# Linear attention and feed-forward layers on one core: another order for every engine's queue

## Chip, core and metric

The kernel runs on one NeuronCore of a Trainium2 chip. The time is what the device takes for one execution, in microseconds (us); several executions are timed and the median is given. Lower is better. The core's engines work side by side, each through a queue of its own in program order: TensorE (PE, with its weight loads as PEld), VectorE (DVE), ScalarE (ACT), GpSimd (POOL), and SyncE (SP), which here issues nearly all transfers.

## The reference

Two kinds of layer alternate, A, B, A, B, on 2048 tokens of width 512 in bf16; both A layers share weights, both B layers too.

```python
def _A_ref(x, wqkv, wo):          # 32 heads of 16
    q, k, v = ...                 # x @ wqkv
    phi = lambda t: jnp.where(t > 0, t + 1, jnp.exp(t)) + 1e-6
    pq, pk = phi(q), phi(k)
    kv = jnp.einsum("bhsd,bhse->bhde", pk, v)
    z = jnp.einsum("bhsd->bhd", pk)
    num = jnp.einsum("bhqd,bhde->bhqe", pq, kv)
    den = jnp.einsum("bhqd,bhd->bhq", pq, z)[..., None] + 1e-6
    ...                           # (num / den) @ wo

def _B_ref(x, w1, w2):            # 512 -> 1376 -> 512
    ...                           # relu(x @ w1) @ w2

x = x + _A_ref(_layernorm(x, axis=-1), A_wqkv, A_wo)
x = x + _B_ref(_layernorm(x, axis=-1), B_w1, B_w2)
x = x + _A_ref(_layernorm(x, axis=-1), A_wqkv, A_wo)
x = x + _B_ref(_layernorm(x, axis=-1), B_w1, B_w2)
```

## The kernel before

The 2048 tokens are 16 tiles of 128, in four chunks of four tiles. Layers are numbered 0 (A), 1 (B), 2 (A), 3 (B), and the steps of a layer are interleaved with those of the next, so that a later layer starts on chunk 0 while the earlier one still works on chunk 3.

A step has a name with the numbers of layer, chunk or tile, and part. In the first A layer a tile goes through `bnst`, `bnag` (statistics, VectorE, lines 846 and 847), `rstd`, `fnorm` (normalization, VectorE, line 884), `trp` (transposition on TensorE, line 913) or `tr` (transposition by DMA, line 899), and `trev` (its copy to SBUF). `kproj`, `qh` and `qproj` are the projections, all issued as matmuls at line 952. `lin` and `exp` (lines 932 and 934, ScalarE) and `em` and `phi` (VectorE) make the feature map. `den`, `lnd`, `rdc`, `spread` (DMA, line 1226) and `pqs` make the division; `g`, `kv`, `kvmask`, `m` and `fin` contract keys with values and apply the output weights; `resid`, `sq`, `nmean` to `nbias` and `norm` are the residual and the next normalization. Many products are computed with seven block products instead of eight: `aqsum` and `aksum` (VectorE, line 1005) subtract blocks of the weights; `q7` and `k7` are the seven products of the projections, `h1` to `h7` and `p1` to `p7` those of the two feed-forward matrices, with the sums of the other operand in `as`, `hs` and `ssum`. In a feed-forward layer `hv` are ScalarE's copies of half-made sums out of PSUM (line 699 seeds a second PSUM bank with such a copy), `hc` the additions and relus, `hr` the last 96 hidden units, `trh` their transposition.

The order of work is not the order of the code. All steps are first collected in a graph, and a planner then makes one queue for each engine. In the graph a step gets a number as it is created, and its place in the queue is that number plus a hint from a table, line 421:

```python
op.prio = op.idx + HINTS.get(op.key, 0)
```

`HINTS` (line 63) has 1,638 such numbers. It has another 264 entries that end in "!": these choose, for a step that two engines could do, one of them. The planner's window is 1 on every engine (line 60), so a queue is simply sorted by place, and a step that waits holds up all that stand behind it. The planner then runs its queues against its own table of durations to find when each of the eight PSUM banks comes free, gives the banks out, and derives the waits from that. `LOAD_LATE` (line 53) is what it adds to the landing times of the early loads in that calculation.

The places that the prediction uses are sums of this kind. On VectorE `bnst4` was created as number 52 and has the hint 17, place 69; `aqsum3` was created as 200 and has -44, place 156. The TensorE steps of the first microseconds stand in this order before: `kproj1_1`, `qh0_0_1_0`, `trp2`, `qh0_0_2_0`, `trp3`, `qh0_0_3_0`, `qh0_0_0_0`, `kproj2`, four `qh` steps, `qh0_0_2_1`, `kproj3`, two `qh` steps, `trp4`.

Of the kernel before, what the change touches and what calls it, by code (L numbers as in the profile page):

```python
# [52 lines left out]
LOAD_LATE = {"x1": 270.0, "x2": 440.0, "wka": 580.0, "wkb": 440.0, "wqa": 600.0, "x4": 1200.0, "wqb": 1160.0, "x12": 960.0, "x8": 760.0, "wv0": 350.0}  # L53
# [9 lines left out]
HINTS = {"0.aqsum1": -69, "0.aqsum1!": 0, "0.aqsum2": -40, "0.aqsum2!": 0, "0.aqsum3": -44, "0.aqsum3!": 0, "0.aqsum4": -12,  # L63
# [327 lines left out]
class _Graph:  # L391
# [19 lines left out]
    def add(self, eng, emit, reads=(), writes=(), dur=100.0, lat=0.0, dma=False, name=""):  # L411
        if eng == ACT and name != "table" and not dma:
# [7 lines left out]
                   POOL: 0 if name.startswith(("ms_", "as", "onec")) else 2 if "norm" in name else 1}  # L420
        op.prio = op.idx + HINTS.get(op.key, 0)
        deps = {}
# [29 lines left out]
    def add_flex(self, alts, reads=(), writes=(), name=""):  # L452
        e0, em0, d0 = alts[0]
        op = self.add(e0, em0, reads, writes, d0, name=name)
        op.alts = list(alts)
        c = HINTS.get(op.key + "!")
        if c is not None and c < len(alts):
# [1516 lines left out]
```

## Time and profile before

| | us |
|---|---|
| median of 3 runs | 263.93 |
| lowest and highest | 262.88, 264.66 |
| the profiled execution | 262.89 |
| its span, first to last instruction | 260.9 |

The profile is of one execution. It lists for each engine when each instruction ran. A line of the timeline gives the start, the time until the last record of the group ends, engine, source line, operation, what is written and read, sizes and count; in brackets stands the idle time before it and what ended it. Matmul records overlap, since the next matmul starts before the last one has drained, so the distance between two starts tells more than the length of a record. The chain is followed back from the last instruction: at each step to what released it.

### The profile page before, as it was taken

How to read it: one execution, taken by the hardware profiler on the slowest of the kernel's cores; microseconds unless marked ns; L12 is line 12 of the kernel's file. 1: busy time of each engine (PE TensorE's matmuls, PEld its weight loads, DVE VectorE, ACT ScalarE, POOL GpSimd, SP SyncE). 2: the span in 40 equal slices, each digit the busy share in tenths (PEclk: the TensorE clock that was granted, in tenths of full speed). 3: DMA queues.
4: the chain of work that ended last, by engine and by line, in shares of the span. 5: the costliest groups of instructions: out<-in, count | busy, mean ns of one | idle time of the engine just before them, and what ended most of it. 6: DMA issues, size and time to landing. Idle time of an engine off the chain costs nothing.

```text
span 260.9 us, 5905 instructions
## 1 busy us (share of the span) xinstructions
PE 255.5 (98%) x2176; PEld 198.3 (76%) x2176; DVE 231.1 (89%) x574; ACT 204.1 (78%) x442; POOL 60.4 (23%) x164
## 2 busy tenths in 40 slices
PE   7999999999999999999999999999999999999995
PEld 2555668734778888898888878774488988988884
DVE  4899999799989999999899999759999999977674
ACT  4899998769989978899998799686999945970200
POOL 4110000018843016340330340002986000000000
PEclk9999999999999999999999999999999999999999
DMA  6757970743432440323021030047442504300104
GB/s 198 285 143 126 322 230 0 186 111 67 85 68 57 60 83 8 75 41 63 0 58 26 0 75 9 3 107 174 92 80 57 102 3 123 60 20 3 80 3 161
DMA packets 45980, 22.46 MB, mean 86 GB/s; under 512 B 35872, under 2 KB 44416, under 8 KB 45952
## 3 DMA queue, kind: packets, MB, share of 16 engines
q1 hardware_dynamic: 45680, 21.83, 34.7%
q8 instruction: 17, 0.28, 0.5%
q10 hardware_dynamic: 272, 0.26, 0.4%
q14 instruction: 11, 0.09, 0.1%
HBM read 7.14 MB, written 2.10 MB: 35 GB/s over the span
## 4 chain that ended last, share of the span: by engine, by line
PE 82%; ACT 6%; DMA 5%; DVE 2%; SPq 2%; issue 2%
PE ps L952 81%; DMA Tb<-xn 3%; ACT sqscr L967 2%; SPq L1226 2%; ACT xn L894 1%; DMA xin<-in_A_x_dram 1%; DMA big<-rdc 1%; PE ps L913 1%; ACT ps L699 1%; ACT rdc L1216 0%; ACT lnd L1214 0%; DVE xn L889 0%; DVE xn L884 0%; DVE bst L846 0%; DVE big L1234 0%
## 5 line engine op out<-in xcount | busy, mean ns | idle before, releaser
L699 ACT ACTIVATE ps<-ps 128x512 f32<-128x512 f32 (+1 forms) x41 | 23.1, 573 | 19.4 <-PE ps L952 17.8
L952 PE MATMUL ps<-big,xn 128*128 128x256 bf16 (+1 forms) x224 | 32.7, 288 | 0.0
L952 PE MATMUL ps<-w,big 128*128 128x256 bf16 (+1 forms) x256 | 32.5, 272 | 0.0
L967 ACT ACTIVATE sqscr<-xres 128x512 bf16<-128x512 f32 x48 | 29.8, 622 | 2.9 <-DVE xres L959 2.2
L952 PE MATMUL ps<-Mf,big 128*128 128x512 bf16 x128 | 28.5, 379 | 0.0
L952 PEld LDWEIGHTS ps<-w,big 128*128 128x128 bf16 (+1 forms) x256 | 25.0, 98 | 3.0
L952 PEld LDWEIGHTS ps<-big,xn 128*128 128x128 f16 x224 | 21.3, 98 | 6.6 <-issue 1.1
L952 PE MATMUL ps<-Tb,w 128*128 128x256 f16 x160 | 24.2, 273 | 0.0
L952 PEld LDWEIGHTS ps<-Mf,big 128*128 128x128 bf16 x128 | 12.2, 98 | 14.6 <-ACT Mf L1165 0.5
L1435 DVE TENSOR_TENSOR big<-ps,escr 128x512 bf16<-128x512 f32 (+1 forms) x38 | 22.5, 600 | 0.9 <-PE ps L952 0.5
L952 PE MATMUL ps<-xn,xin 128*128 128x256 f16 x160 | 23.0, 273 | 0.1
L952 PE MATMUL ps<-xn,w 128*128 128x256 f16 x160 | 22.9, 273 | 0.0
L868 POOL TENSOR_SCALAR mean<-s 128x2 f32<-128x2 f32 x24 | 8.9, 377 | 54.9 <-DVE xres L959 53.7
L952 PE MATMUL ps<-wqkv,Tb 128*128 128x512 bf16 (+1 forms) x96 | 20.6, 344 | 0.0
L1423 ACT ACTIVATE big<-ps 128x512 bf16<-128x512 f32 (+1 forms) x37 | 20.2, 563 | 0.3 <-DVE xn L1401 0.2
L894 ACT ACTIVATE xn<-xres,nbias,rstd 128x512 f16<-128x512 f32 x24 | 19.5, 830 | 0.5 <-DVE nbias L878 0.5
L1454 ACT ACTIVATE escr<-ps 128x512 f32<-128x512 f32 (+1 forms) x38 | 19.2, 541 | 0.4 <-PE ps L952 0.2
L876 POOL TENSOR_TENSOR rstd<-veps,nhalf 128x2 f32<-128x2 f32 x24 | 18.0, 750 | 4.5 <-DVE veps L874 4.0
L952 PE MATMUL ps<-w,Tb 128*128 128x96 bf16 (+2 forms) x176 | 17.3, 224 | 0.2 <-DMA Tb<-xn 0.2
L952 PEld LDWEIGHTS ps<-Tb,w 128*128 128x128 bf16 x160 | 15.5, 98 | 2.2 <-DVE w L1383 0.3
L952 PEld LDWEIGHTS ps<-xn,w 128*128 128x128 bf16 x160 | 15.5, 98 | 2.0
L952 PEld LDWEIGHTS ps<-xn,xin 128*128 128x128 bf16 x160 | 15.2, 98 | 2.2 <-ACT ps L699 0.4
(146 smaller groups left out, 627.8 us busy)
## 6 DMA issues: line engine op xcount, KB each, us to landing
big<-rdc SPq DMA_DIRECT2D x32, 128.0 KB, 2.7
xin<-in_A_x_dram SPq DMA_DIRECT2D x3, 512.0 KB, 7.5
w<-in_B_w_dram SPq DMA_DIRECT2D x1, 1376.0 KB, 7.1
w<-in_B_w_dram SPq DMA_DIRECT2D x1, 1280.0 KB, 10.5
wqkv<-in_A_wqkv_dram SPq DMA_DIRECT2D x3, 256.0 KB, 5.0
wqkv<-in_A_wqkv_dram SPq DMA_DIRECT2D x1, 512.0 KB, 4.3
wo<-in_A_wo_dram SPq DMA_DIRECT2D x1, 512.0 KB, 4.3
out_dram<-GT SPq DMA_DIRECT2D x1, 512.0 KB, 2.6
```

Of the source, the lines that this page charges most:

```text
L699: g.add(ACT, lambda e: e.activation(psv[:, b, 0:w], psv[:, src, 0:w], ACTF.Identity), [("ps", src)], [("ps", b)], C_ACT_PSUM if w == 512 e ...
L868: g.add(POOL, lambda e: e.tensor_scalar(mean[:, sl], s1[:, sl], -INV_D, None, ALU.mult), [("s1", i) for i in tl], [("mean", i) for i in tl ...
L876: g.add(POOL, lambda e: e.tensor_tensor(rstd[:, sl], veps[:, sl], nhalf[:, 0:n], ALU.pow), [("veps", lo), ("nhalf",)], [("rstd", i) for i ...
L894: (ACT, lambda e: e.activation(xn[:, i, :], src, ACTF.Identity, scale=rstd[:, i:i + 1], bias=nbias[:, i:i + 1]), C_ACT_SB_AP)],
L913: last = e.transpose(psb()[:, 128 * c:128 * c + 128], xn[:, i, 128 * c:128 * c + 128], ident[:])
L952: last = e.matmul(o, l, r, start=st, stop=sp, skip_group_check=skip)
L967: g.add(ACT, lambda e: e.activation(sqscr[:, q, :], xres[:, i, :], ACTF.Square, scale=math.sqrt(INV_D), accum_out=s2[:, i:i + 1]), xr(i), ...
L1226: dma(lambda e, j=j, u=u: e.dma_start(unit_ap(u), rdc[32 * j:32 * j + 32, t, :].unsqueeze(1).broadcast_to([32, 4, 512])), [("rdc", t)], [( ...
L1423: g.add_flex([(ACT, lambda e: e.activation(ap, src(), ACTF.Relu), C_ACT_PSUM if w == 512 else 270.0), (DVE, lambda e: e.tensor_scalar(ap, ...
L1435: g.add(DVE, lambda e: e.tensor_tensor(ap, sh(psv[:, bank, 0:w]), sh(other()), ALU.add), [("ps", bank)] + okeys + ([] if first else bk), q ...
L1454: g.add(ACT, lambda e, w=w: e.activation(q[:, 0:w], psv[:, bank, 0:w], ACTF.Identity), [("ps", bank)], key, C_ACT_PSUM if len(cs) == 2 els ...
```

## The change

Only two tables are changed: `LOAD_LATE`, and the numbers in `HINTS`. The keys of the tables are the same; 1,418 of the 1,638 place numbers and 50 of the 264 choices of engine differ. No instruction is added or removed; 50 small steps (evacuations, relus, additions, parts of the normalization) go to the other engine that can do them. Cut to what the prediction speaks of:

```diff
-LOAD_LATE = {"x1": 270.0, "x2": 440.0, "wka": 580.0, "wkb": 440.0, "wqa": 600.0, "x4": 1200.0, "wqb": 1160.0, "x12": 960.0, "x8": 760.0, "wv0": 350.0}
+LOAD_LATE = {"x1": 320.0, "x2": 490.0, "wka": 780.0, "wkb": 540.0, "wqa": 1000.0, "x4": 1300.0, "wqb": 1260.0, "x12": 1060.0, "x8": 960.0, "wv0": 350.0}
...
-HINTS = {"0.aqsum1": -69, "0.aqsum1!": 0, "0.aqsum2": -40, "0.aqsum2!": 0, "0.aqsum3": -44, "0.aqsum3!": 0, "0.aqsum4": -12,
+HINTS = {"0.aqsum1": -43, "0.aqsum1!": 0, "0.aqsum2": -24, "0.aqsum2!": 0, "0.aqsum3": -126, "0.aqsum3!": 0, "0.aqsum4": 36,
...
-         "0.qc7_3_22_exp": -14, "0.qh0_0_0_0": -43, "0.qh0_0_0_1": -10, "0.qh0_0_1_0": -59, "0.qh0_0_1_1": -36,
+         "0.qc7_3_22_add": -21, "0.qc7_3_22_exp": -14, "0.qh0_0_0_0": -54, "0.qh0_0_0_1": -6, "0.qh0_0_1_0": -63,
...
-         "1.h5_0_0": 18, "1.h5_0_2": 12, "1.h5_0_4": 19, "1.h5_1_0": 7, "1.h5_1_2": -5, "1.h5_1_4": -10, "1.h5_2_0":
+         50, "1.h4_3_2": 60, "1.h4_3_4": 60, "1.h5_0_0": 18, "1.h5_0_2": 11, "1.h5_0_4": 18, "1.h5_1_0": -8,
...
-         "1.hc11_3_2!": 0, "1.hc11_3_4": 61, "1.hc11_3_4!": 0, "1.hc12_0_0": 37, "1.hc12_0_2": 45, "1.hc12_0_4": 52,
+         "1.hc12_0_0": 34, "1.hc12_0_2": 38, "1.hc12_0_4": 52, "1.hc12_1_0": 26, "1.hc12_1_2": 28, "1.hc12_1_4": 37,
...
-         "1.hs1_1": -18, "1.hs1_2": -52, "1.hs1_3": -120, "1.hs2_0": 26, "1.hs2_1": -9, "1.hs2_2": -25, "1.hs2_3":
+         "1.hrrelu2!": 0, "1.hrrelu3": 4, "1.hrrelu3!": 0, "1.hs1_0": 18, "1.hs1_1": -13, "1.hs1_2": -47, "1.hs1_3":
...
-         -96, "2.q7_2_2": -60, "2.q7_2_3": -33, "2.q7_2_4": 1, "2.q7_2_5": -46, "2.q7_2_6": -42, "2.q7_2_7": -11,
+         "2.q7_2_3": -38, "2.q7_2_4": 0, "2.q7_2_5": -45, "2.q7_2_6": -42, "2.q7_2_7": -22, "2.q7_3_1": -75,
```

Sorted by the new places, the first TensorE steps read `qh0_0_1_0`, `kproj1_1`, `qh0_0_0_0`, `trp2`, `trp3`, `qh0_0_3_0`, `kproj2`, seven `qh` steps, `kproj3`, `qh0_0_2_1`, `trp4`: the same number of matmuls ahead of `trp4`. VectorE reads `bnst4`, `aqsum3`, `bnag4`, `fnorm6`, `veps4`, `fnorm7`, `bnst5`, `fnorm4`. On SP the four spreads of chunk 0 stand ahead of the load `w2b` and the transposition of chunk 2's first half ahead of `trh0`; the loads up to x8 keep their order. The first steps of TensorE up to `kproj1_0`, and of VectorE up to `bnst4`, are unchanged.

593 rows, old and new, of the table HINTS are left out of this document.

## The prediction

> **What bounds the kernel now.** I read the page's busy shares first, then the chain that ended last, then the windows by stage, and then the timeline of TensorE alone at each place where the chain leaves it.
>
> ```profile
> span 260.9 us, 5905 instructions
> PE 255.5 (98%) x2176; PEld 198.3 (76%) x2176; DVE 231.1 (89%) x574; ACT 204.1 (78%) x442; POOL 60.4 (23%) x164
> L952 PE MATMUL ps<-Mf,big 128*128 128x512 bf16 x128 | 28.5, 379 | 0.0
> ```
> ```profile
> 76.00 73.59 PE ps L952 x690
> ...
> 151.34 3.48 DMA Tb<-xn
> 154.81 0.05 issue
> 154.86 103.43 PE ps L952 x924
> 258.29 0.02 issue
> 258.32 0.42 DVE rdc L1609
> ```
> ```profile
> 16.00:42.00 26.00, 26.00 (x170) 15.97 (x170) 25.92 (x71) 26.00 (x57) 0.56 (x3) 1.00 0.68 193
> 217.00:258.00 41.00, 41.00 (x396) 36.58 (x395) 32.42 (x64) 15.44 (x33) 0.00 (x0) 1.00 0.22 59
> ```
>
> A busy share of 98% proves little, since matmuls overlap in the records: the mean record of the 512-column form is 379 ns, while 128 of them fill only 28.5 us, 223 ns each. So I go by the distance from one start to the next. The last leg of the chain is 924 matmuls in 103.43 us, 112 ns each, without one step off the engine. The windows (PE, PEld, DVE, ACT and POOL busy, then granted clock, DMA) say the same at a clock of 1.00. They also show that from 16 to 42 us VectorE (25.92 of 26.00) and ScalarE (26.00) have nothing left either, while from 217 to 258 us both have room. TensorE is the bound; an order of queues can only win where TensorE waits.
>
> **How much waiting there is.** The spacings first, then the waits. TensorE from 8 to 14 us:
>
> ```profile
> 8.32 0.38 PE L952 MATMUL ps<-Tb,wqkv 128*128 128x256 f16 x2
> 9.09 0.40 PE L913 MATMUL ps<-ident,xn 128*128 128x128 f16 x4 [0.38 <-DVE xn L884]
> 9.32 0.38 PE L952 MATMUL ps<-Tb,wqkv 128*128 128x256 f16 x2
> 9.54 0.39 PE L913 MATMUL ps<-ident,xn 128*128 128x128 f16 x4
> 9.76 0.60 PE L952 MATMUL ps<-Tb,wqkv 128*128 128x256 f16 x4
> 10.20 1.03 PE L952 MATMUL ps<-wqkv,Tb 128*128 128x512 bf16 x4
> 11.06 1.25 PE L952 MATMUL ps<-Tb,wqkv 128*128 128x256 f16 x10
> 12.15 1.03 PE L952 MATMUL ps<-wqkv,Tb 128*128 128x512 bf16 x4
> 13.02 0.60 PE L952 MATMUL ps<-Tb,wqkv 128*128 128x256 f16 x4
> 13.65 0.40 PE L913 MATMUL ps<-ident,xn 128*128 128x128 f16 x4
> ```
>
> Ten matmuls of 256 columns lie between 11.06 and 12.15: 0.109 us each. Four of 512 lie between 12.15 and 13.02: 0.217 each. By these the pair at 8.32 is issued by 8.54 and the next step, `trp2`, starts at 9.09: a wait of 0.55. The four at 13.02 are out by 13.46 and `trp4` starts at 13.65: 0.19. The later waits, first the two around 75 us (TensorE, then VectorE, then ScalarE), then those near 154 and near 52 us (TensorE, and VectorE's step between):
>
> ```profile
> 74.04 0.38 PE L952 MATMUL ps<-Tb,w 128*128 128x256 f16 x2
> 74.63 0.84 PE L952 MATMUL ps<-w,Tb 128*128 128x96 bf16 x16 [0.21 <-DMA Tb<-xn]
> 75.30 0.60 PE L952 MATMUL ps<-Tb,w 128*128 128x256 f16 x4
> 76.00 0.83 PE L952 MATMUL ps<-xn,xin 128*128 128x256 f16 x6
> ```
> ```profile
> 74.51 0.42 DVE L1401 TENSOR_TENSOR xn<-Tb 128x512 f16<-128x512 f16 x1 [0.87 <-DMA Tb<-xn]
> 74.86 0.68 DVE L1435 TENSOR_TENSOR big<-ps,escr 128x512 bf16<-128x512 f32 x1
> ```
> ```profile
> 75.58 0.37 ACT L699 ACTIVATE ps<-ps 128x256 f32<-128x256 f32 x1 [0.73 <-DVE big L1435]
> ```
> ```profile
> 153.77 1.03 PE L952 MATMUL ps<-big,xn 128*128 128x512 bf16 x4
> 154.86 0.61 PE L952 MATMUL ps<-Tb,wqkv 128*128 128x256 f16 x4
> ```
> ```profile
> 52.18 0.59 PE L952 MATMUL ps<-Mf,big 128*128 128x512 bf16 x2
> 52.86 0.60 PE L952 MATMUL ps<-wo,KVT 128*128 128x512 bf16 x2
> ```
> ```profile
> 52.38 0.42 DVE L1158 TENSOR_TENSOR KVT<-ps,bmask 128x256 bf16<-128x256 f32 x1 [0.34 <-PE ps L952]
> ```
>
> In the same way: `hr1_0` waits 74.63 - 74.26 = 0.37 for the transposed chunk; `h6_0_4` waits 76.00 - 75.74 = 0.26 for ScalarE's copy at 75.58, which waited for VectorE's addition at 74.86, which stood behind `hs1_1`, which waited 0.87 for the same transposition; `q7_3_1` waits 154.86 - 154.64 = 0.22 for the transposition issued at 151.34; `m2` waits 52.86 - 52.61 = 0.25 for `kvmask1`. Together 0.55 + 0.19 + 0.37 + 0.26 + 0.22 + 0.25 = 1.84 us. That is all that I find worth the name, and it is 0.7% of 262.89: a new order that removed every one of them would not be faster by 1%.
>
> **The change part by part.** Nothing is added or removed; every price is a wait that goes, moves or appears. `LOAD_LATE` emits nothing: it only feeds the planner's clock, and reaches the program through the banks and the waits it chooses.
>
> *The start, SP and loads.* The order of the ten loads is the same, so x and the weights should land as before. On TensorE `qh0_0_0_0` moves from behind `trp3` to ahead of `trp2` (its place number falls from 62 to 51): two matmuls, 0.22 us, go into the wait of 0.55. That saves nothing by itself, because the next wait down the queue, `trp4` at 13.65, is set by VectorE:
>
> ```profile
> 9.70 1.29 DVE L846 BATCH_NORM_STATS2 bst<-xin 128x6 f32<-128x512 bf16 x2 [0.35 <-DMA xin<-in_A_x_dram]
> 11.12 0.66 DVE L846 BATCH_NORM_STATS2 bst<-xin 128x6 f32<-128x512 bf16 x1
> 11.82 0.18 DVE L847 BATCH_NORM_AGGREGATE mv<-bst 128x2 f32<-128x6 f32 x1
> 12.60 0.68 DVE L846 BATCH_NORM_STATS2 bst<-xin 128x6 f32<-128x512 bf16 x1
> 13.20 0.40 DVE L884 TENSOR_SCALAR xn<-xin,mv,rstd 128x512 f16<-128x512 bf16 x1
> ...
> 17.62 0.41 DVE L1005 TENSOR_TENSOR Mf<-wqkv 128x512 bf16<-128x512 bf16 x1
> 17.96 1.05 DVE L884 TENSOR_SCALAR xn<-xin,mv,rstd 128x512 f16<-128x512 bf16 x3
> ```
>
> From the landing of x4 (9.70) to `fnorm4` (13.20 to 13.60) VectorE has no gap, and `trp4` follows 0.05 behind. Into this run the change puts `aqsum3` (place 156 before, 74 after; `bnst4` 68, `bnag4` 77). The trace has its twin at 17.62, whose successor starts 0.34 later. So `fnorm4` ends at 13.94 and `trp4` starts at 13.99: +0.34. Queued behind `aqsum3` are `bnag4`, `fnorm6`, `fnorm7` and the transposition of their tiles, all later by the same 0.34, so nothing there is lost twice. TensorE has as much work ahead of `trp4` as before, so it cannot pay this back; it only waits longer (0.19 + 0.22 + 0.34 = 0.75). Bounds: nothing, if in a usual run x4 lands so that a hole is there for `aqsum3`; 0.41, its whole record. I take +0.34.
>
> *16 to 42 us.* VectorE is rid of that 0.34, TensorE had no wait to lose, no engine choice flips here. I take 0. The cover is the two full engines beside it; the price if it tears is the second rival.
>
> *42 to 60 us.* The one `fin` step between `kv1_3` and `m2` is exchanged for another (`fin2_0` for `fin0_0`), both two matmuls, and `kvmask1` keeps its place: the 0.25 stays. The spreads of the first chunk now pass `ld_w2b` on SP, whose data are first read far later: 0. `m0` comes closer to `kvmask0`, two steps of four 256-column matmuls (0.87) behind `kv0_3`, where the `m2` row shows that 0.43 + 0.25 = 0.68 are needed: 0.
>
> *74 to 76 us.* Ahead of `hr1_0` stand the same steps as before and `norm6` keeps its neighbours: 0.37 stays. But `hc12_0_2` now stands ahead of `hs1_1` on VectorE (517 against 525; before 524 against 520), so its 0.87 holds up nobody, and on TensorE `h5_1_0` (536) passes `h6_0_4` (539): four matmuls, 0.44, more than the wait. -0.26. SP puts `trh0` behind a transposition of chunk 2; its reader `p1_0_0` comes some fifteen TensorE steps later, and I take 0.
>
> *149 to 155 us.* `q7_2_7` (place 62 before, 51 after) goes ahead of `q7_3_1`: 0.44 of work in front of a wait of 0.22; the queue that makes the transposition is in the same order. -0.22. *The last layer* is shuffled as much as the rest, but its final VectorE steps and stores are the same in kind, and the 0.42 at 258.32 stays the end.
>
> Named terms: +0.34 - 0.26 - 0.22 = -0.14. Beside them, some hundreds of steps trade places and 50 small steps change engine. That exposes waits which no row shows, since each depends on banks and evacuations. From below: none (it cannot gain where TensorE has no gap). From above: as many as the old order has after 16 us (four: 0.25, 0.37, 0.26, 0.22, together 1.10). Two of those four are dissolved here; I take it that two others replace them, at their mean of 0.28, and halve the 0.55 since the last stage has room on both other engines: +0.3. Sum: +0.16, call it +0.2.
>
> Against the profiled run: 262.89, of which 260.9 is the span and 2.0 lies around it, gives 263.1. The median of the runs, 263.93, stands 1.04 above the profiled run; the trace does not say where, so I leave that distance as it is: **264.1**.
>
> **The rivals.**
> *Almost all waits go:* the named gains count, the start costs nothing because x4 lands in another rhythm, and 74.63 shrinks too: -0.26 - 0.22 - 0.37 = -0.85, 263.1; at the very best -1.84, 262.1. For it: the waits are few and small. Against: the gapless VectorE run from 9.70. Chance 0.16.
> *VectorE or ScalarE loses time between 16 and 42 us:* one queue's head waits for a product or a transposition that now comes later, and with 25.92 and 26.00 of 26.00 busy nothing regains it. The price of one such wait is the 0.87 of `hs1_1`; three chunks are evacuated in this stage, 3 x 0.87 = 2.6, so 266.7. It decides from the point where the idle time exceeds the 0.34 that `aqsum3` leaves free. Against: TensorE has no gap at all there now. Chance 0.12.
> *TensorE's spacing itself gives way* beside other neighbours. If the 128 matmuls at 223 ns went at the 109 ns of half their width, 128 x 0.114 = 14.6 us would go: 249.5. Against: both spacings hold wherever no wait is shown. Chance 0.02. The Trainium skill, "TensorE: Matmul & The Clock Gate", section "Back-to-back issue gap", gives about 131 ns a matmul for a sustained stream of 512 columns; the 217 ns between 12.15 and 13.02 disagree, and the trace decides.
> *The change does nothing:* the moved steps lie under cover everywhere, 263.9. Chance 0.08. The forecast has the remaining 0.62.
>
> **How the numbers follow.** 1% is 2.6 us, about what a measurement of this kernel can tell from no change. Faster by that needs the spacing rival: 0.02, and 0.01 for what no case covers. Slower: the second rival, 0.12. Within: 0.85. The forecast's own range is 263.4 (no new wait, start +0: -0.48) to 265.0 (start +0.41, all 1.10 of new waits: +1.03). To hold 8 in 10 it takes in the first rival, down to 262.7, and the smaller half of the second, up to 265.8.
>
> **What would show it.** Right: `trp4` at about 14.0 behind a longer wait, no TensorE gap before the step that was `h6_0_4` and before `q7_3_1`, one of about 0.37 still before `hr1_0`, 0.25 before `m2`. Wrong: `trp4` still at 13.65; a gap in TensorE between 16 and 42 us; several new gaps of over 0.3 after 80 us; or a chain whose last leg is no longer TensorE alone.

## The result, and the profile after

| us | before | after |
|---|---|---|
| median of 9 runs each | 263.61 (262.67 to 264.95) | 262.21 (261.68 to 262.97) |
| ratio of the runs, 95% interval | | 0.9945 (0.9919 to 0.997) |
| again, 29 and 12 runs on another occasion | 263.09 (262.32 to 264.76) | 262.42 (261.60 to 263.28) |
| ratio, 95% interval | | 0.9959 (0.9935 to 0.9983) |
| the profiled execution, its span | 262.89, 260.9 | 262.21, 260.5 |

The change is faster by 0.4 to 0.55% (the ratios take all runs; the medians are 1.40 and 0.67 us apart), and its executions lie closer together. The forecast, 264.1 with 262.7 as its lower end, missed it; that the difference would stay under 1% held. The two profiled executions differ by only 0.68 us, of which 0.4 lie in the span. So part of the gain may lie in executions of the kernel before that its first profile does not show.

The page of the changed kernel, its chain of waits around 70 us and its windows (PE, PEld, DVE, ACT and POOL busy, granted clock, DMA):

```profile
span 260.5 us, 5888 instructions
PE 255.3 (98%) x2176; PEld 198.9 (76%) x2176; DVE 230.7 (89%) x574; ACT 207.5 (80%) x446; POOL 60.0 (23%) x160
```
```profile
70.18 4.40 DMA Tb<-xn
74.58 0.14 issue
74.71 183.07 PE ps L953 x1674
257.79 0.02 issue
257.81 0.43 DVE rdc L1610
```
```profile
16.00:42.00 26.00, 26.00 (x172) 15.79 (x170) 25.70 (x69) 25.90 (x56) 0.67 (x3) 1.00 0.65 190
```

TensorE is the bound as before. Its last unbroken leg is now 183 us long and starts at `hr1_0`, behind a DMA transposition of 4.40 us; before, the leg began at 154.86. Between 16 and 42 us the two full engines stayed full and TensorE kept its pace. TensorE at the four places of the prediction (the start, near 52, near 74 and near 154 us), then VectorE's run from the landing of x4:

```profile
8.23 0.38 PE L953 MATMUL ps<-Tb,wqkv 128*128 128x256 f16 x2
8.78 0.72 PE L914 MATMUL ps<-ident,xn 128*128 128x128 f16 x8 [0.16 <-DVE xn L885]
...
13.17 0.38 PE L953 MATMUL ps<-Tb,wqkv 128*128 128x256 f16 x2
13.39 0.39 PE L914 MATMUL ps<-ident,xn 128*128 128x128 f16 x4
...
51.87 0.59 PE L953 MATMUL ps<-Mf,big 128*128 128x512 bf16 x2
52.55 0.61 PE L953 MATMUL ps<-wo,KVT 128*128 128x512 bf16 x2
...
73.70 0.38 PE L953 MATMUL ps<-xn,w 128*128 128x256 f16 x2
74.71 0.84 PE L953 MATMUL ps<-w,Tb 128*128 128x96 bf16 x16 [0.64 <-DMA Tb<-xn]
75.39 0.60 PE L953 MATMUL ps<-Tb,w 128*128 128x256 f16 x4
75.83 0.82 PE L953 MATMUL ps<-xn,xin 128*128 128x256 f16 x6
...
153.96 1.03 PE L953 MATMUL ps<-big,xn 128*128 128x512 bf16 x4
154.82 0.60 PE L953 MATMUL ps<-Tb,wqkv 128*128 128x256 f16 x4
```
```profile
9.18 1.29 DVE L847 BATCH_NORM_STATS2 bst<-xin 128x6 f32<-128x512 bf16 x2
...
10.61 0.66 DVE L847 BATCH_NORM_STATS2 bst<-xin 128x6 f32<-128x512 bf16 x1
11.18 0.41 DVE L1006 TENSOR_TENSOR Mf<-wqkv 128x512 bf16<-128x512 bf16 x1
11.51 0.17 DVE L848 BATCH_NORM_AGGREGATE mv<-bst 128x2 f32<-128x6 f32 x1
...
12.88 0.40 DVE L885 TENSOR_SCALAR xn<-xin,mv,rstd 128x512 f16<-128x512 bf16 x1
```

By the distances from start to start: the wait before `h6_0_4` is gone (75.83 follows 75.39 by 0.44, the time of four matmuls), so is the one before `q7_3_1` (0.86 for four of 512 columns), and 0.25 before `m2` stays. But `hr1_0` now waits 74.71 - 73.92 = 0.79, where 0.37 was to stay. And `aqsum3` stands where the prediction put it, at 11.18, yet `trp4` starts at 13.39, not at 14.0 (x4 also landed earlier here, at 9.16 in place of 9.68).

### The profile page after: what moved, and what is told of

Same layout as the page of the kernel before. It is cut to its first block, busy times and chain, and to the rows that moved or that the text cites. A ratio compares the mean times of both kernels' runs of the same rounds, so it can differ in the third digit from the quotient of the medians.

```text
span 260.5 us, 5888 instructions
## 1 busy us (share of the span) xinstructions
PE 255.3 (98%) x2176; PEld 198.9 (76%) x2176; DVE 230.7 (89%) x574; ACT 207.5 (80%) x446; POOL 60.0 (23%) x160
## 4 chain that ended last, share of the span: by engine, by line
PE 85%; ACT 5%; DVE 4%; DMA 4%; SPq 1%; issue 1%
PE ps L953 84%; DVE xres L960 2%; DMA Tb<-xn 2%; SPq L1227 1%; ACT sqscr L968 1%; DMA big<-rdc 1%; DMA xin<-in_A_x_dram 1%; ACT xn L895 1%; DVE bst L847 1%; PE ps L914 0%; ACT rdc L1217 0%; DVE big L1235 0%; ACT escr L935 0%; ACT ps L700 0%; ACT lnd L1215 0%
## 5 line engine op out<-in xcount | busy, mean ns | idle before, releaser
L953 PE MATMUL ps<-big,xn 128*128 128x256 bf16 (+1 forms) x224 | 32.1, 288 | 0.0
L869 POOL TENSOR_SCALAR mean<-s 128x2 f32<-128x2 f32 x24 | 7.2, 301 | 54.4 <-DVE xres L960 52.8
L1424 ACT ACTIVATE big<-ps 128x512 bf16<-128x512 f32 (+1 forms) x38 | 18.9, 527 | 0.4 <-PE ps L953 0.3
L1445 ACT ACTIVATE big<-big 128x1024 bf16<-128x1024 bf16 (+1 forms) x16 | 14.3, 904 | 3.5 <-DVE big L1436 3.3
```

Of the source, the lines that this page charges most:

```text
L869: g.add(POOL, lambda e: e.tensor_scalar(mean[:, sl], s1[:, sl], -INV_D, None, ALU.mult), [("s1", i) for i in tl], [("mean", i) for i in tl ...
L953: last = e.matmul(o, l, r, start=st, stop=sp, skip_group_check=skip)
L1424: g.add_flex([(ACT, lambda e: e.activation(ap, src(), ACTF.Relu), C_ACT_PSUM if w == 512 else 270.0), (DVE, lambda e: e.tensor_scalar(ap, ...
L1445: g.add_flex([(ACT, lambda e: e.activation(row, row, ACTF.Relu), 945.0 if len(cs) == 2 else C_ACT_SB), (DVE, lambda e: e.tensor_scalar(row ...
```

## The experiments

Waits of TensorE below are distances from start to start, less the usual one for the width (217 ns for 512 columns, 109 for 256, 42 for 96). Each kernel was also timed beside the kernel before, if not called a profiled run alone.

**Where does the gain sit, and was the first profile of before a typical one?** Two kernels with half of the new numbers each, and a second profiled run of each of the pair, without an edit.

```diff
-"0.aqsum1": -69
+"0.aqsum1": -43
...
-"1.h5_1_0": 7
+"1.h5_1_0": -8
...
 "2.q7_2_7": -11
 "2.q7_3_1": -78
```

That is the first, with the new numbers for layers 0 and 1 and the old ones for 2 and 3; the second is the reverse.

> The first two layers take the new order, the last two keep the old one; nothing is computed otherwise. Theory A (the gain is a wait here and there, spread over the kernel): about half of the gain, 0.5 to 0.8 us faster than before, and the wait near 154 us before q7_3_1 is still there with 0.2 us. Theory B (the old order loses time in a usual execution near the start, where transfers land at changing times, and the profiled execution of before was a lucky one): nearly the whole gain, 1.0 to 1.4 us faster. Theory C (the gain lies in the last two layers, whose order changed as much): within 0.3 us of before.

> The last two layers take the new order, the first two keep the old one; nothing is computed otherwise. Theory A: 0.4 to 0.8 us faster than before. Theory B: only the wait of 0.22 us before q7_3_1 goes, 0.1 to 0.3 us faster. Theory C: 1.0 to 1.4 us faster.

> The kernel before, unchanged, for a second profiled execution. Theory B: the loads land at other times than in the first profile by some tenths of a us, and the waits of TensorE come out larger than the 1.84 us found there, by up to 0.8 us. Theories A and C: the same waits within 0.2 us.

> The changed kernel, unchanged, for a second profiled execution. Theory B: its waits vary less from profile to profile than those of the kernel before, within 0.4 us in sum. Theories A and C: as little as those of the kernel before.

New orders in layers 0 and 1 alone: 263.72 us, ratio to the kernel before 1.0026 (1.0002 to 1.005). In layers 2 and 3 alone: 267.23 us, 1.0159 (1.0123 to 1.0195). Neither half carries the gain, and both are slower than either whole. TensorE in the second, where the steps of layer 1 in their old order meet layer 2 in its new one:

```profile
120.48 1.27 PE L952 MATMUL ps<-w,big 128*128 128x256 bf16 x10 [0.80 <-ACT ps L699]
...
127.33 0.39 PE L952 MATMUL ps<-w,big 128*128 128x256 bf16 x2 [0.94 <-DVE xres L1601]
```

Neither wait is in the kernel before or after. The first half, too, has a wait that neither whole has, 0.78 us near 145.6. So these two runs suggest that the order of one layer is made for that of the next, and say nothing about where the gain lies.

The second profiles said more. The kernel before took 264.35 us, 1.46 more than in its first profile, the changed one 263.17. The start, where theory B looked for the loss, is not the place: `trp4` started at 13.67 in this profile of the kernel before, at 13.65 in the first. The chain of waits of this second profile of the kernel before, and TensorE there:

```profile
70.72 5.36 DMA Tb<-xn
```
```profile
74.30 0.38 PE L952 MATMUL ps<-Tb,w 128*128 128x256 f16 x2
76.21 0.84 PE L952 MATMUL ps<-w,Tb 128*128 128x96 bf16 x16 [1.53 <-DMA Tb<-xn]
```

The transposition that `hr1_0` waits for landed 5.36 us after its issue, 4.05 in the first profile, and the wait was 1.69 us, not 0.37. That is nearly the whole difference between the two executions. What delays it shows in the DMA queues. From 70 to 75 us, first the first profile of before, then this one (queue, kind: packets, MB, share of the time of 16 DMA engines):

```profile
q8 instruction: 1, 0.02, 1.7%
q14 instruction: 1, 0.01, 0.4%
```
```profile
q14 instruction: 1, 0.01, 2.1%
q8 instruction: 1, 0.02, 1.1%
```

These are blocks of the program itself, fetched while it runs: 16 KB on one queue, 8 KB on the other. The 8 KB block took 0.3 us in the first profile (0.4% of 80 us) and 1.65 us in the second, where its packet starts 0.26 us after that of the 16 KB block, which took 0.89. In the first profile it came first. Both fall on the packets of the transposition, which run from 1.2 us after its issue. This became theory F: TensorE's wait depends on when two instruction fetches come.

**Moving TensorE's fetches.** The warm-up matmuls at the start were cut into more, narrower ones of the same total width, so that TensorE's instructions are counted on but no queue changes its order. The changed kernel was timed again beside them.

```diff
-                for k in range(WARM):
-                    last = e.matmul(psv[:, wt, :], wrm[:, 0:128], wrm[:, :], start=True, stop=True)
+                for w in [112] * 32 + [128] * 4:
+                    last = e.matmul(psv[0:64, wt, 0:w], wrm[:, 0:64], wrm[:, 0:w], start=True, stop=True)
```

With 16 more matmuls the list is `[168] * 16 + [176] * 8`.

> The changed kernel once more, timed beside the kernel before on one chip. Theory F (instruction fetches): around 72 us TensorE's 16 KB instruction fetch and an 8 KB fetch of another engine travel while the DMA transposition that hr1_0 waits for is under way; in the kernel before both overlap it, its landing varies (4.05 to 5.36 us after its issue in three profiles) and with it the wait of TensorE there (0.37 to 1.69 us); in the changed kernel only one overlaps it (4.27 to 4.51 us, waits of 0.80 to 1.12 us). F expects a median near 262.3, some 0.7 under the kernel before, and a narrower spread (under 1.5 us against over 2). Theory O (order): the gain is the two waits that the new order removes for good, 0.26 us near 76 us and 0.2 us near 154 us; O expects 0.5 us and the same spread for both.

> The kernel before with its eight warm-up matmuls of 512 columns cut into 36 narrower ones of the same total width: 28 more matmuls, so every later fetch of TensorE's instructions comes some 3 us earlier; every queue keeps its order. F expects the 16 KB fetch of 73.4 us before 70.6 us, the transposition issued at 70.4 to land within 3.4 us, the wait before hr1_0 under 0.1 us, a median some 0.8 us under the kernel before (262.2 where that has 263.0) and the tail of executions over 263.6 gone. O, or any cause other than the fetch, expects the wait before hr1_0 between 0.4 and 1.7 us as before and a ratio of 1.000 +- 0.0015.

> The changed kernel with its warm-up matmuls cut into 24 of the same total width: 16 more, so TensorE's fetches come some 1.7 us earlier. F expects the fetch of 72.0 us near 70.3, before the packets of the transposition start near 71.4, the transposition to land 3.1 to 3.4 us after its issue in place of 4.4, the wait before hr1_0 under 0.2 us in place of 0.8 to 1.1, and a median near 261.4, 0.8 under the changed kernel. O expects the changed kernel's time, 262.2 +- 0.3.

> The changed kernel with the warm-up cut into 36 matmuls of the same total width: 28 more, TensorE's fetches some 3 us earlier, the one of 72.0 near 69 us. F expects it clear of the transposition that hr1_0 waits for, as in the kernel with 16 more, but now on the one issued near 67.4, which has some 1 us of slack; a median of 261.2 to 261.8. O expects the changed kernel's time, 262.2 +- 0.3.

The changed kernel again: 0.9959. The three others: the kernel before with 28 more matmuls 266.03 us, 1.0094 (1.0059 to 1.0129); the changed one with 16 more 264.18, 1.0029 (1.0007 to 1.0051); with 28 more 263.94, 1.0025 (0.9996 to 1.0054). F was right about the place in part, and wrong about the sum. In the kernel before with 28 more, the 16 KB fetch came 2.49 us before the issue of the transposition, but the 8 KB one stayed at 2.52 us after it; it landed after 3.88 us, where F expected at most 3.4, and `hr1_0` waited 0.13. In the changed kernel with 28 more, the 16 KB fetch came 2.75 us before the issue of the transposition, which then landed after 3.04 us, and TensorE passed `hr1_0` without a wait:

```profile
73.99 0.38 PE L953 MATMUL ps<-xn,w 128*128 128x256 f16 x2
74.21 0.84 PE L953 MATMUL ps<-w,Tb 128*128 128x96 bf16 x16
```

But the other fetches had moved too, onto other transfers. In the kernel before with 28 more and in the changed one with 16 more, TensorE stood still at places where neither had a wait worth the name (below, the transposition and TensorE behind it, in each of the two):

```profile
80.42 4.71 DMA Tb<-xn
```
```profile
85.17 0.61 PE L952 MATMUL ps<-Tb,w 128*128 128x256 f16 x4 [1.27 <-DMA Tb<-xn]
```
```profile
12.47 5.10 DMA Tb<-xn
```
```profile
17.61 0.60 PE L953 MATMUL ps<-wqkv,Tb 128*128 128x512 bf16 x2 [1.60 <-DMA Tb<-xn]
```

A 16 KB fetch starts 2.04 us after the issue of the first of these transpositions and 2.89 us after that of the second; in the first profiles of the pair, without a fetch on them, the same two landed after 3.06 and 3.26 us. So cutting the warm-up matmuls differently, with no other change, costs 1.5 to 2.9 us in the median here. With 16 more the 16 KB fetch before `hr1_0` did not come earlier against the transposition than without them (0.95 us after its issue; 0.32 to 1.80 in the four profiles of the changed kernel); why stays open.

**The named moves alone, the start undone, the wait filled.** The kernel before with the two moves of the prediction that paid, the changed kernel with `aqsum3` back, the changed kernel with two products ahead of `hr1_0`, and a third profiled run of the kernel before:

```diff
-"1.h5_1_0": 7, "1.h6_0_4": 46, "1.hc12_0_2": 45, "1.hs1_1": -18, "2.q7_2_7": -11, "2.q7_3_1": -78
+"1.h5_1_0": -8, "1.h6_0_4": 49, "1.hc12_0_2": 38, "1.hs1_1": -13, "2.q7_2_7": -22, "2.q7_3_1": -75
```
```diff
-"0.aqsum3": -126
+"0.aqsum3": -44
```
```diff
-"1.h2_0_4": 64, "1.h6_0_4": 49, "1.hv1_0_4": 45
+"1.h2_0_4": 39, "1.h6_0_4": 37, "1.hv1_0_4": 41
```

> The kernel before with the two local moves of the change alone: near 76 us hc12_0_2 ahead of hs1_1 on VectorE and h5_1_0 ahead of h6_0_4 on TensorE; near 154 us q7_2_7 ahead of q7_3_1 on TensorE. All other orders as before. Theory O (the lasting gain is these two moves): the 0.26 us wait before h6_0_4 and the 0.16 to 0.23 us wait before q7_3_1 are gone, from hr1_0 to den0 of the third layer 94.3 us in place of 94.7 to 94.8, a median 0.4 to 0.5 under the kernel before, and the wait before hr1_0 still anywhere between 0.37 and 1.7 us, so that the spread stays over 2 us. Rival S (only the orders together do it): as in the kernels with half of the new orders, new waits eat the gain; no faster than before.

> The changed kernel with aqsum3 back at its old place on VectorE, after bnag7; nothing else differs. My prediction charged that step 0.34 us by way of fnorm4 and trp4. If that holds, trp4 starts 0.34 us earlier against the landing of x4 and the median is 0.2 to 0.3 under the changed kernel. If the step filled a gap between bnst4 and bnag4 (0.13 us before), 0.2. If other waits of the first 17 us bind, no change to the start of kproj6.

> The changed kernel with two products that do not need the transposition, h2_0_4 and h6_0_4, ahead of hr1_0 on TensorE, and hv1_0_4 ahead of hc21_0_0 on ScalarE, which makes their banks ready. F: the wait before hr1_0 (0.60 to 1.12 us in three profiles) is partly filled, 0.2 to 0.44 us of work moved into it; a median 0.2 to 0.4 under the changed kernel. If the two products now wait for hv1_0_4 themselves and hr1_0 starts later than the landing, nothing is gained.

> One more look at the kernel before. F expects the wait before hr1_0 at 0.37 us when the transposition lands 4.05 us after its issue, and 1.3 us more when the two fetches overlap on it; the span minus this wait within 0.3 us of 260.6.

The two moves in the old order: 263.84 us, 1.0043 (1.0014 to 1.0072), slower. TensorE there, near 75 and 157 us:

```profile
75.13 0.60 PE L952 MATMUL ps<-Tb,w 128*128 128x256 f16 x4
75.67 1.26 PE L952 MATMUL ps<-xn,xin 128*128 128x256 f16 x10
...
156.19 0.60 PE L952 MATMUL ps<-big,xn 128*128 128x256 bf16 x4
157.03 0.61 PE L952 MATMUL ps<-Tb,wqkv 128*128 128x256 f16 x4 [0.24 <-ACT ps L699]
```

The old waits go (0.26 before `h6_0_4` becomes 0.10), and others take their place: 0.22 and 0.24 us up to 77.87 and 78.99, 0.40 before 157.03, where ScalarE's seed is late. Rival S holds: among the old neighbours the two moves are worth less than nothing. Among the new ones the waits that they were to remove are gone, 0.44 us on the mean of the profiles below; no run took the moves out of the changed kernel.

`aqsum3` back at its place: 262.62 us, 0.9974 (0.9952 to 0.9995), not faster than the changed kernel; `trp4` at 13.79, which is the mean of the changed kernel too. The products ahead of `hr1_0`: 262.37, 0.9969 (0.9947 to 0.9992), no measurable gain. In its profile `hr1_0` no longer waits, but the first of the two does, 0.45 us for ScalarE's copy.

The third profiled run of the kernel before: 264.37 us, landing after 5.36 us, wait 1.62 us. Span less wait, 262.4 - 1.6, is 260.8, as expected.

**Moving VectorE's fetches.** One-column memsets on VectorE while it waits for x:

```diff
-        wrm = sb("wrm", [128, 512], BF16)
+        wrm, pad = sb("wrm", [128, 512], BF16), sb("pad", [128, 16], BF16)
...
-        g.add(DVE, lambda e: e.memset(wrm[:], 0.0), [], [("wrm",)], 150, name="ms_wrm")
+        g.add(DVE, lambda e: [e.memset(wrm[:] if k == 0 else pad[:, k:k + 1], 0.0) for k in range(11)][0], [], [("wrm",)], 150, name="ms_wrm")
```

> The kernel before with ten one-column memsets on VectorE after its first one, at 1.2 us, where VectorE has nothing to do until 2.9 us. No queue changes its order; VectorE's instruction fetches come ten instructions earlier. F (two fetches on one transposition): VectorE's fetch, 2.3 to 2.5 us after the issue of the transposition near 70.4, moves to before its packets start at 1.2 us after the issue; the landing is never 5.36 us after the issue, at most 4.1; TensorE's wait before hr1_0 at most 0.4 us; the group of executions over 263.1 thins out and the median falls by 0.5 to 0.9 us against the kernel before, ratio 0.9965 to 0.998. Rival C (the long landing comes from something else, such as the memory side of the transposition): landing and spread as before, ratio 1.000 +- 0.0015.

> The kernel before with three such memsets: VectorE's fetch some 0.7 us earlier, still on the packets of the transposition (1.2 to 3 us after its issue). F expects the two groups of executions and the median of the kernel before, 1.000 +- 0.0015, and a landing at 4.0 or near 5.4 us. If the added memsets themselves help, or shift something at the start, it looks like the kernel with ten.

> The changed kernel with five such memsets: VectorE's fetch, 3.3 to 3.9 us after the issue of the transposition, comes some 1.2 us earlier, next to TensorE's fetch while the packets are under way. F expects landings over 5 us in some executions and the wait before hr1_0 up to 1.9 us, so a median 0.3 to 0.9 us over the changed kernel, near 263, and a spread over 2 us. C expects the changed kernel's time, 262.4, and landings of 4.0 to 4.5 us.

With ten: 263.11 us, 0.9998 (0.9973 to 1.0023). The DMA queues from 72 to 74 us, first of before, then of this kernel, and its TensorE:

```profile
q8 instruction: 1, 0.02, 4.2%
q14 instruction: 1, 0.01, 1.0%
```
```profile
q8 instruction: 1, 0.02, 3.8%
```
```profile
74.46 0.38 PE L952 MATMUL ps<-Tb,w 128*128 128x256 f16 x2
74.68 0.84 PE L952 MATMUL ps<-w,Tb 128*128 128x96 bf16 x16
...
153.48 1.03 PE L952 MATMUL ps<-big,xn 128*128 128x512 bf16 x4
155.02 0.61 PE L952 MATMUL ps<-Tb,wqkv 128*128 128x256 f16 x4 [0.51 <-DMA Tb<-xn]
```

The 8 KB fetch had left the transposition (1.64 us before its issue), which landed after 3.05 us, and `hr1_0` had no wait. That is as F had it. But 0.67 us were lost before `q7_3_1`, where before loses 0.2, and the runs went from 262.07 to 264.87 as those of before do. F expected a ratio of 0.9965 to 0.998; the mechanism at its place is shown, its weight in the median is not.

With three: 263.26 us, 0.9991 (0.9965 to 1.0016). The fetch moved not by 0.7 but by more than 3 us, so this was no control. The 16 KB fetch alone lay on the transposition and it landed after 4.67 us, with 0.92 of wait: one fetch is enough. With five in the changed kernel: 262.76, 0.9962 (0.9941 to 0.9983), no change. The fetch near 74 us stayed 3.85 us behind the issue, so this run tells nothing about F.

**The pair once more, and the wait filled further.** In the third, `hv1_0_4` now also passes `hv1_1_0`:

```diff
-"1.hv1_0_4": 41
+"1.hv1_0_4": 34
```

> One more look at the kernel before. TensorE's waits from 68 to 82 us together either 0.6 to 0.8 us (landing 4.0 us after the issue) or 1.9 to 2.0 us (landing near 5.4 us); the wait before q7_3_1 0.16 to 0.25 us. If the pair differs elsewhere, the sum is under 0.6 us and the time still over 263.

> One more look at the changed kernel. TensorE's waits from 68 to 82 us together 0.6 to 1.2 us, landing 4.0 to 4.5 us after the issue and never over 5; no wait before q7_3_1; the time 261.6 to 263.2.

> The changed kernel with h2_0_4 and h6_0_4 ahead of hr1_0, and hv1_0_4 now ahead of hv1_1_0 too, so that it can start when h1_0_4 ends. In the first version of this TensorE still waited 0.45 us for hv1_0_4 (74.39 where 73.94 was free). Expected: that wait 0.25 us, TensorE's waits from 68 to 82 us together 0.3 to 0.7 us in place of 0.6 to 1.2 us, median 0.2 to 0.5 under the changed kernel, ratio to the kernel before 0.994 to 0.996. If a wait for ScalarE comes after hr1_0 in its place (h2_1_0 for hv1_1_0), no gain.

The kernel with the wait filled further took 262.70 us, 0.9959 (0.9936 to 0.9982), again the time of the changed kernel: it waits 0.41 us for ScalarE there, and `hr1_0` none. No version of mine beat it. With the two last there are four profiles of each kernel; x4 to `trp4` counts from the landing of the load:

| profile | us | transposition lands after | TensorE waits 68 to 82 | before `q7_3_1` | before `m2` | x4 to `trp4` |
|---|---|---|---|---|---|---|
| before, first | 262.89 | 4.05 | 0.72 | 0.23 | 0.25 | 3.98 |
| second | 264.35 | 5.36 | 2.03 | 0.16 | 0.25 | 4.24 |
| third | 264.37 | 5.36 | 1.92 | 0.16 | 0.25 | 4.37 |
| fourth | 262.69 | 4.09 | 0.78 | 0.16 | 0.25 | 4.57 |
| after, first | 262.21 | 4.40 | 0.91 | 0 | 0.25 | 4.23 |
| second | 263.17 | 4.51 | 1.16 | 0 | 0.25 | 4.44 |
| third | 262.46 | 4.13 | 0.63 | 0 | 0.25 | 4.39 |
| fourth | 262.67 | 3.40 | 0.03 | 0 | 1.18 | 4.17 |

The fourth profile of the changed kernel missed its expectation: no wait at `hr1_0`, but 1.2 us before `m2`. Its chain and TensorE there:

```profile
47.75 4.69 DMA big<-rdc
```
```profile
52.27 0.59 PE L953 MATMUL ps<-Mf,big 128*128 128x512 bf16 x2
53.88 0.39 PE L953 MATMUL ps<-wo,KVT 128*128 128x512 bf16 x1 [1.02 <-DVE KVT L1159]
```

A spread that took 2.62 to 2.99 us in the other three took 4.69, VectorE stood behind it, and with it `kvmask1`. The profile of the run with `aqsum3` back has the same loss, 1.04 us before `m2`, and there the spread is

```profile
47.66 4.58 DMA big<-rdc
```

A 16 KB instruction fetch starts at 50.41 in the fourth profile, 2.66 us after the issue of that spread, and 2.54 us after it in the other run. But in the three profiles without the loss one starts 2.24 to 2.53 us after it. So the changed kernel has a place of its own where such a loss comes and goes; that the fetch makes it is likely, but not shown.

## Why the prediction was wrong, point by point

The means of the four profiled runs are 263.58 and 262.63 us, 0.95 apart. By place: waits from 68 to 82 us 1.36 and 0.68, so -0.68; before `q7_3_1` -0.18; before `m2` +0.23; near 63 us -0.09 (0.16 and 0.07); the start 0. And -0.24 outside the span, on which below. That sums to -0.96. The forecast for the change was +0.16, and the 1.12 between them are these terms: the start 0.34, the wait before `hr1_0` that was to stay 0.42, the time outside the span 0.24, the place near 63 us 0.09, the new waits 0.07, and -0.04 for `q7_3_1`.

*The step that failed is the last of the sum:* "the median of the runs, 263.93, stands 1.04 above the profiled run; the trace does not say where, so I leave that distance as it is". It carried a property of the old order over to the new one: the changed kernel's medians, 262.21 and 262.42, stand 0 and 0.21 above its first profile. In part the distance was the draw of three runs: on five later occasions, with 17 or 29 executions each, the median of the kernel before was 262.95 to 263.92. The rest is in how its executions spread: of 130 timed ones of the kernel before, on six occasions, 65 took longer than 263.28, which is the longest of 23 of the changed kernel. One place of it is known: in the old order the transposition before `hr1_0` can be hit by two fetches, and the first profile was one of the cheap cases. In the six traces with the old order at that place and its 8 KB fetch unmoved, the fetch starts 2.3 to 2.5 us after the issue, under the packets, and two of the six land after 5.36 us. In those two the 16 KB fetch came 0.26 and 0.39 us ahead of it; in the other four the 8 KB fetch came first or alone, and the transposition landed after 3.88 to 4.09. In the eleven traces with the new order there, it starts 2.6 to 3.9 us after it, and none lands later than 4.51. The term "0.37 stays" fell with it: that wait was a draw, 0.37 to 1.69 before, 0 to 1.1 after.

That this place carries the median is read from these profiles and not shown by an intervention: the kernel whose transposition was freed in the old order did not become faster, and its runs still went up to 264.87. So it stays open what the long executions wait for in general, and how much of the gain would remain with other fetch positions.

*"262.89, of which 260.9 is the span and 2.0 lies around it":* I took the 2.0 as fixed. It is 1.98 us for the kernel before (mean of 29 executions) and 1.74 for the changed one (12), with a standard deviation of 0.03 in both. It follows the last two layers: 1.75 with only their order new, 2.06 with only that of the first two. What of the ending does it was not tried.

*The start, +0.34:* the named cost is not there on the mean. `trp4` starts at 13.77 on the mean before and 13.79 after. `aqsum3` does go into the run from x4, and fills the 0.13 us that `bnag4` had waited for `bnst4`. That makes the run 0.21 longer, not 0.34. And the run sets `trp4` only where TensorE is through with what stands ahead of it: in the first profile of before (3.98 us after the landing of x4) and in the fourth of the changed kernel (4.17). In the other six what stands ahead is later. Undoing the step gained nothing that could be measured. The bound "nothing" was nearest.

*16 to 42 us, 0:* right. *42 to 60 us, 0:* right in three profiles of four, and not in the fourth (1.18 before `m2`).

*74 to 76 us, -0.26, and 149 to 155 us, -0.22:* right in kind and size. The wait before `h6_0_4` is in every profile of the kernel before and in none of the changed one, the one before `q7_3_1` measured 0.18 on the mean. But the working behind them was incomplete: the same six numbers in the old order gain nothing, since other waits take the place of these. The gain belongs to the moves together with the steps around them.

*New waits, +0.3:* after 80 us there are none; what is new is the longer wait before `m2` in one profile of four, +0.23 on the mean, so the size was near and the reason another. *`LOAD_LATE`:* as said, it emits nothing; with the new hints the planner makes the same program from either table.

*"1% [...] about what a measurement of this kernel can tell from no change":* the intervals reach 0.25% to either side, so a change of half of 1% could be told.

The rival nearest to the outcome is that almost all waits go (263.1, at best 262.1). The measured time lies between its two figures, but not for its reason: the waits as a whole did not go. From 68 to 82 us TensorE waits 0.91 us in the first profile of the changed kernel, 0.72 in that of the kernel before. What is no longer seen is the long case of one wait, so the nearness of that figure is luck.

## What to carry to other kernels

One profile of a kernel whose runs spread by 1% is a draw. Before a wait that ends with a DMA landing is priced at what one trace shows, look at it in several, and ask where the distance between the profiled run and the median sits. In a kernel as full as this, an order is worth what it is worth as a whole: three parts of a better order, put into the old one, each made it slower.

## What the runs showed of the hardware

The program's own blocks travel with the data. Here TensorE's come as 16 KB on one queue, 17 times in the span, about every 125 matmuls, and took 0.88 to 1.9 us; 28 more matmuls at the start moved the first from 17.6 to 12.1 us. On another queue come blocks of 8 KB, in 0.31 us at the least and in 1.65 to 1.7 close behind a 16 KB one; some of them moved when VectorE had ten more instructions (the one at 72.75 us to 69.23), so these are VectorE's, and others stayed. The transposition before `hr1_0`, 3.04 us without a fetch on its packets, mostly took 3.9 to 4.7 with one or with both (3.40 in one profile), and 5.36 where the 8 KB block came 0.26 or 0.39 us behind the 16 KB one. Elsewhere one 16 KB fetch was enough for 5.10. Not every fetch under way delayed it: one of 16 KB that began 2.52 us after the issue left it at 3.05, one of 8 KB at 2.61 left it at 3.04, while another of 8 KB at 2.52 had it at 3.88.

The Trainium skill, "Runtime: NRT & Kernel Launch", section "Instruction fetch mechanics", says that each engine's sequencer fetches its next block of 16 KiB (256 instructions) over a DMA queue of its own and that this is mostly hidden. The traces agree on TensorE's 16 KB. They differ on the 8 KB of the other queue, and on the hiding: TensorE itself keeps its pace through its fetches (six of them between 82 and 154 us in the first profile of before, and no wait over 0.13 us there), but a data transfer beside a fetch was late by up to 2.3 us, and TensorE waited for it.
